# A forgetting-attention plus feed-forward kernel on Trainium2: splitting the second GEMM of chunk 0 over the attention of two batches

## The chip, the cores and the metric

The kernel runs on one core of one Trainium2 chip. The metric is device time in microseconds (us); lower is better. Every run named below computed the right result.

## The reference, cut to what matters

Eight batches of causal attention with a decay ("forget gate") are followed by a feed-forward block with an exact GELU. All inputs and outputs are float32.

```python
# q, k, v: (8 batches, 8 heads, 576 tokens, 64);  f: (8, 8, 576)
scores = q @ k.T / 8 + cum[:, :, :, None] - cum[:, :, None, :]   # cum = cumsum(log f)
attn   = softmax(where(causal, -1e9, scores))
x      = (attn @ v) -> (4608 tokens, 512)
h      = x @ w_in                       # 512 -> 2048, "first GEMM"
out    = gelu(h) @ w_out                # 2048 -> 512, "second GEMM"
```

## The kernel before

The kernel is a hand-made schedule: the order of the Python calls is the order of the instructions on each engine. A *chunk* is 512 of the 576 tokens of a batch (the 64-token tails of all batches form a ninth chunk at the end). For each batch there is an *attention* stage of 16 *score tiles* (four head pairs i, four tiles t), followed by the *first GEMM* of its chunk (16 blocks of four matmuls, each evacuated by a Gelu on ScalarE). The *second GEMM* of the chunk before is cut into *units* of one 128x128x512 matmul (or its equal) each, 64 in a chunk, and these fill the gaps of the attention.

In batch 0 and batch 1 q and k are transposed on TensorE (`transposes_pe`), and VectorE copies the result, eight copies for each group of two heads:

```python
    def transposes_pe(b, i, pool):
        ...                                   # 12 small matmuls into two PSUM tiles
        for which, ps in enumerate(pss):
            for h in range(2):
                ...
                for odd in range(2):
                    nc.vector.tensor_copy(rows[:, odd], ps[odd * D : (odd + 1) * D, h]...)
```

Batch 1 is attended with the second GEMM of chunk 0 as its filler. The lists give the number of units after each score tile:

```python
    FILL_1 = [[0, 4, 4, 0], [0, 2, 3, 3], [4, 4, 4, 4], [3, 3, 3, 3], [8, 0, 99]]

    def second_attention():
        b, fill, counts = 1, gemm2(0, True), FILL_1
        for i in range(HP):
            for t in range(4):
                scores(b, i, t)
                if i and t == 1:
                    attend(b, i - 1, 0, (0, 1, 2))
                ...                            # heads of pair i-1 at t = 2 and 3
                    if i < HP - 1:
                        x_dma(b, i - 1)        # x transposed by a DMA
                if (i, t) == (0, 2):
                    transposes_pe(1, 3, o_psum)
                if i == 1 and t in (0, 2):
                    weigh_v(1, 2 + t // 2)
                ...                            # loads of v and transposes of batch 2
                take(fill, counts[i][t])
        ...
```

The loads of w_out and the transposes of batch 1 stand in the first GEMM of chunk 0:

```python
        if b == 0:
            load_w_out(0)
            x_tail_dma(0)
        for ffb in range(0 if b else 4, n_ff):
            gemm1(b, ffb)
            if b == 0:
                if ffb in (7, 9, 15):
                    transposes_pe(1, (7, 9, 15).index(ffb), s_psum if ffb < 10 else o_psum)
                if ffb == 9:
                    weigh_v(1, 0)
                    for c in range(1, 4):
                        load_w_out(c)
                    load_qk_tokens(2)
                    weigh_v(1, 1)
            elif b + 1 < B:
                ...                            # copies and weighing for the next batch
```

The q,k of batch 1 are requested earlier, on the same GpSimd queue as w_in:

```python
        load_qk_tokens(1, 0, 4)
        load_w_in(2)
        load_w_in(3)
        load_qk_tokens(1, 4, 8)
```

The softmax here doesn't subtract the row's maximum and nothing guards it: scores larger than these inputs give would overflow.

## Time and profile before

| | kernel before |
|---|---|
| time, median of 3 runs | 356.26 us (354.95 to 357.58) |
| span of the profiled run | 356.0 us (an execution of 358.29 us) |
| first GEMM of chunk 0 starts | 26.66 us |
| attention of batch 1, with 64 units | 43.4 to 76.75 us |
| attention of batch 2, with 64 units | 90.66 to about 113.6 us |
| first score tile of batch 3 | 127.45 us |

The profile is one execution, and a slow one: at 358.29 us it lies above the three timed runs, with a mean granted clock of 0.986. Of the 38 fast runs of this kernel beside the experiments, the 20 at a clock of 0.993 or more average 354.2 us and the 6 at 0.986 or less 357.8 us. So the waits and the half clock of this trace need not be in every run. PE is TensorE, DVE VectorE, ACT ScalarE, POOL GpSimd, and SP issues many of the DMAs. A line of the timeline gives start and duration in us, engine, source line, operation, output<-input, and in brackets the idle time ahead of it with what ended that. A line of the waits gives engine and tile, the releaser, total us, number of waits, and the longest. The lines themselves stand in the prediction.

### The profile page before, as it was taken

The page shows a single profiled execution, that of the slowest core. Times are in us where ns is not written, and L with a number is a line of the kernel's source. Part 1 is how long each engine was busy: PE and PEld are TensorE (multiplying, and loading weights), DVE is VectorE, ACT ScalarE, POOL GpSimd, SP SyncE. Part 2 cuts the span into 40 slices and gives each one's busy share as a digit, 9 for nine tenths or more (in the row PEclk, how much of TensorE's full clock was granted, in tenths as well). Part 3 has the DMA queues.
Part 4 walks back from the last instruction along what each step waited for, and adds up shares of the span by engine and source line. Part 5 has one row for each costly group of instructions (what it writes and reads, how often), then busy time and mean ns, then how long its engine had stood idle before and what let it go on. Part 6 is the DMA issues. An engine that isn't in the chain of part 4 may idle for free.

```text
span 356.0 us, 7788 instructions
## 1 busy us (share of the span) xinstructions
PE 336.3 (94%) x3090; PEld 176.1 (49%) x3132; DVE 204.1 (57%) x503; ACT 215.1 (60%) x296; POOL 125.5 (35%) x245
## 2 busy tenths in 40 slices
PE   7698949999999999999999999999999999999995
PEld 3574523454555445544554455445544555444443
DVE  4561972579458955695669656974698363011011
ACT  5966563626874787478756876577647874603600
POOL 8291624334344424451446143705360430000000
PEclk9989996999999999999999999999999999999999
DMA  7899999955997779367945894389910121011013
GB/s 117 167 153 199 195 120 201 180 116 149 179 175 173 126 138 211 93 105 135 224 107 86 145 218 124 64 146 202 153 47 0 46 62 66 2 59 59 2 29 88
DMA packets 101219, 43.24 MB, mean 121 GB/s; under 512 B 80000, under 2 KB 96640, under 8 KB 101184
## 3 DMA queue, kind: packets, MB, share of 16 engines
q1 hardware_dynamic: 83888, 28.60, 40.2%
q0 software_dynamic: 16896, 13.63, 26.2%
q8 instruction: 24, 0.39, 0.5%
q10 hardware_dynamic: 400, 0.52, 0.4%
q14 instruction: 11, 0.09, 0.1%
HBM read 36.85 MB, written 9.44 MB: 130 GB/s over the span
## 4 chain that ended last, share of the span: by engine, by line
PE 76%; DMA 8%; ACT 7%; POOL 4%; SPq 3%; issue 2%; DVE 0%; POOLq 0%; ACTq 0%
PE ps L401 31%; PE ps L490 17%; PE ps L441 12%; PE o L338 9%; PE s L311 6%; DMA v_sb<-in_v_dram 4%; ACT e L317 4%; DMA w_out_sb<-in_moe_w_out_dram 4%; SPq L114 3%; ACT L317 2%; POOL vw L285 1%; ACT g L414 1%; PE ps_x L376 1%; POOL q L102 1%; POOL k L102 1%
## 5 line engine op out<-in xcount | busy, mean ns | idle before, releaser
L414 ACT ACTIVATE g<-ps 128x512 bf16<-128x512 f32 x144 | 85.8, 597 | 82.7 <-PE ps L401 82.7
L317 ACT ACTIVATE e<-s 128x896 bf16<-128x896 f32 (+1 forms) x128 | 103.8, 863 | 37.0 <-PE s L311 36.6
L401 PE MATMUL ps<-xT,w_in_sb 128*128 128x512 bf16 x503 | 111.8, 379 | 1.5 <-ACT g L414 1.0
L319 POOL TENSOR_SCALAR_AFFINE_SELECT e<-e 128x256 bf16<-128x256 bf16 x135 | 53.6, 406 | 123.9 <-ACT e L317 122.7
L490 PE MATMUL ps<-w_out_sb,g 64*128 64x512 bf16 (+1 forms) x666 | 96.2, 376 | 1.0
L401 PEld LDWEIGHTS <-w_in_sb 128*128 128x128 bf16 x576 | 56.0, 98 | 68.2 <-issue 3.0
L285 POOL TENSOR_TENSOR vw<-v_sb,wT 128x640 bf16<-128x640 f32 x32 | 40.9, 1279 | 41.8 <-DMA v_sb<-in_v_dram 25.7
L311 PE MATMUL s<-qT,kT 64*128 64x320 bf16 (+4 forms) x384 | 47.7, 285 | 3.7 <-ACT e L317 3.2
L490 PEld LDWEIGHTS <-g 64*128 64x128 bf16 (+1 forms) x690 | 37.7, 94 | 25.5 <-issue 1.6
L441 PE MATMUL ps<-w_out_sb,g 128*128 128x512 bf16 (+2 forms) x200 | 44.9, 371 | 5.4 <-DMA w_out_sb<-in_moe_w_out_dram 2.7
L338 PEld LDWEIGHTS <-e 128*128 128x128 bf16 x960 | 36.9, 100 | 18.8 <-issue 12.3
L338 PE MATMUL o<-vw,e 128*128 128x65 bf16 x960 | 42.9, 197 | 1.8 <-POOL vw L291 0.9
L269 DVE COPY qT<-tq 64x288 bf16<-64x288 bf16 x96 | 43.4, 452 | 1.5
L498 DVE COPY ot<-ps 128x512 f32<-128x512 f32 x24 | 16.5, 689 | 35.9 <-PE ps L490 35.9
L450 DVE COPY ot<-ps 128x512 f32<-128x512 f32 (+2 forms) x13 | 8.4, 650 | 48.9 <-PE ps L441 46.0
L269 DVE COPY kT<-tk 64x288 bf16<-64x288 bf16 x96 | 34.0, 354 | 1.6
L311 PEld LDWEIGHTS <-kT 64*128 64x128 bf16 x384 | 20.2, 94 | 28.6 <-issue 16.6
L353 DVE RECIPROCAL r<-o 128x5 f32<-128x5 f32 x64 | 12.5, 195 | 37.0 <-PE o L338 36.0
L441 PEld LDWEIGHTS <-g 128*128 128x128 bf16 x208 | 19.0, 99 | 24.2 <-issue 3.8
L354 DVE TENSOR_TENSOR x<-o,r 128x256 bf16<-128x256 f32 x64 | 27.2, 425 | 2.2
L364 DVE TENSOR_SCALAR xt<-o,r 64x64 bf16<-64x64 f32 x60 | 17.4, 291 | 1.4
L500 DVE TENSOR_TENSOR ot<-ot,ps 128x512 f32<-128x512 f32 x24 | 16.5, 688 | 1.3
(65 smaller groups left out, 146.9 us busy)
## 6 DMA issues: line engine op xcount, KB each, us to landing
out_dram<-ot SPq DMA_DIRECT2D x32, 256.0 KB, 2.4
v_sb<-in_v_dram SPq DMA_DIRECT2D x20, 256.0 KB, 4.9
v_sb<-in_v_dram SPq DMA_DIRECT2D x29, 128.0 KB, 5.7
q<-in_q_dram POOLq DMA_DIRECT2D x6, 576.0 KB, 6.1
k<-in_k_dram POOLq DMA_DIRECT2D x6, 576.0 KB, 8.7
w_in_sb<-in_moe_w_in_dram POOLq DMA_DIRECT2D x4, 512.0 KB, 8.6
w_out_sb<-in_moe_w_out_dram POOLq DMA_DIRECT2D x4, 512.0 KB, 16.4
q<-in_q_dram POOLq DMA_DIRECT2D x4, 144.0 KB, 4.4
```

The source lines that it names most:

```text
L269: nc.vector.tensor_copy(rows[:, odd], src[odd * D : (odd + 1) * D, 2 * i + h].rearrange("d j p -> d p j"),)
L285: nc.gpsimd.tensor_tensor(vw_of[b][:, hs, :, 0:D], v_sb[:, hs, :, :], w.unsqueeze(3).to_broadcast([P, 2, NBLK, D]), Alu.mult,)
L311: nc.tensor.matmul(to, *ab, start=half < 0, stop=half == 1 or not masked)
L317: nc.scalar.activation(et[:, :, 0:c], st[:, :, 0:c], Act.Exp, scale=scale)
L319: nc.gpsimd.affine_select(out=et[:, :, c0 : c0 + P], in_=et[:, :, c0 : c0 + P], compare_op=Alu.is_ge, fill=0.0, base=0, pattern=[[0, 2], [ ...
L338: nc.tensor.matmul(o[:, m, :], e_of[b, i, t][:, h, c : c + P], vw_of[b][:, 2 * i + h, n, :], start=(n == 0), stop=(n == m),)
L354: nc.vector.tensor_tensor(x_of[b, i][:, :, h, :], o[:, 0:4, 0:D], r[:, 0:4].unsqueeze(2).to_broadcast([P, NBLK - 1, D]), Alu.mult,)
L364: nc.vector.tensor_scalar(*tail, r[D:P, 4:5], None, Alu.mult)
L401: nc.tensor.matmul(ps, w_in_sb[:, kt, ffb * P : (ffb + 1) * P], src[:, kt, :], start=(kt == 0), stop=(kt == n_dm - 1),)
L414: nc.scalar.activation(g_of[c][ffb], ps, Act.Gelu)
L441: nc.tensor.matmul(pss[ts][:, c0:c1], g_of[c][kt][:, ts * P : (ts + 1) * P], w_out_sb[:, kt, c0:c1], start=(kt == 0), stop=(kt == n_ff - 1),)
L490: nc.tensor.matmul(banks[r], g_of[c][kt][rows, ts * P : (ts + 1) * P], w_out_sb[rows, kt, :], start=(kt == 0), stop=last if r else kt == n ...
```

## The change

The intent is to make the w_out load harmless. In batch 1 TensorE waits twice for w_out. The change leaves only a quarter of the second GEMM of chunk 0 there (16 units, late in the stage, needing half of w_out) and moves the other 48 units into batch 2. That allows q,k of batch 2 to be requested ahead of half of w_out. Around this several things move: v and w_in start earlier, q,k of batch 1 follow all of w_in, the transposes of batch 1 come later, x of batch 1 is transposed on TensorE instead of by DMA, and the first GEMM of chunk 1 gets the interleaved start that chunk 0 has.

```diff
-    FILL_1 = [[0, 4, 4, 0], [0, 2, 3, 3], [4, 4, 4, 4], [3, 3, 3, 3], [8, 0, 99]]
+    FILL_2 = [[8, 8, 8, 8], [8, 8, 4, 4], [4, 4, 4, 4], [4, 4, 4, 4], [8]]
+    FILL_1 = [[0, 0, 0, 0], [0, 0, 0, 0], [0, 0, 2, 2], [2, 2, 0, 0], [4]]
...
-        fill = gemm2_rows(b - 1)
+        fill = gemm2_third() if b == 2 else gemm2_rows(b - 1, PLAN)
...                                            # in the start of batch 0
+        weigh_v(0, 0, nc.vector)
...
-        load_qk_tokens(1, 0, 4)
         load_w_in(2)
         load_w_in(3)
+        load_qk_tokens(1, 0, 4)
         load_qk_tokens(1, 4, 8)
...                                            # in the attention of batch 1
-        b, fill, counts = 1, gemm2(0, True), FILL_1
+        b, fill = 1, gemm2_half(0, 0)
...
+                if (i, t) in ((0, 1), (1, 0)):
+                    transposes_pe(b, 2 + i, o_psum)
...
+                if i and t == 3:
+                    to_xT(b, i - 1, nc.vector.tensor_copy, o_psum, "o")
+                if (i, t) in ((1, 2), (2, 0)):
+                    weigh_v(1, i + 1)
...
+        both = s_psum.tile([P, 2, 1024], BF16, tag="s", name="ps_x2")
+        take(fill, 99)
+        gemm1_begin(1, both)
+        x_tail_dma(1)
+        transpose_dma(2, 0, 4)
         transpose_dma(2, 4, 8)
-        load_v(2, 4, 8)
-        take(fill, 999)
+        load_v(2)
...                                            # in the first GEMM of chunk 0
-            load_w_out(0)
             x_tail_dma(0)
...
-                if ffb in (7, 9, 15):
+                if ffb in (13, 15):
+                    transposes_pe(1, (13, 15).index(ffb), s_psum)
-                if ffb == 9:
+                if ffb == 12:
                     weigh_v(1, 0)
-                    for c in range(1, 4):
-                        load_w_out(c)
+                    load_w_out(0)
+                    load_w_out(1)
+                    weigh_v(1, 1)
                     load_qk_tokens(2)
-                    weigh_v(1, 1)
+                    load_w_out(2)
+                    load_w_out(3)
```

## The prediction

> **What bounds the kernel now.** I read the busy table and the chain of waits first. They name TensorE almost everywhere, so a change can gain only where TensorE stands idle or runs at half clock.
>
> ```profile
> PE 336.3 (94%) x3090; PEld 176.1 (49%) x3132; DVE 204.1 (57%) x503; ACT 215.1 (60%) x296; POOL 125.5 (35%) x245
> ...
> PE 76%; DMA 8%; ACT 7%; POOL 4%; SPq 3%; issue 2%; DVE 0%; POOLq 0%; ACTq 0%
> ```
>
> Next I cut the run into stages with the windows view. In a row stand the stretch, its length, each engine's busy time, then TensorE's granted clock, DMA share and GB/s.
>
> ```profile
> 26.66:43.40 16.74, 15.67 (x102) 7.85 (x102) 9.11 (x21) 10.61 (x18) 6.76 (x10) 1.00 1.24 196
> 43.40:76.75 33.35, 27.41 (x270) 13.25 (x273) 17.87 (x46) 16.27 (x19) 13.16 (x26) 0.90 1.11 158
> 76.75:90.66 13.91, 13.85 (x63) 6.16 (x65) 13.38 (x33) 8.96 (x15) 4.69 (x7) 1.00 0.65 147
> 90.66:113.71 23.05, 22.53 (x289) 13.18 (x293) 12.22 (x33) 16.06 (x19) 9.31 (x22) 1.00 1.07 187
> ```
>
> The rows are the first GEMM of chunk 0, the attention of batch 1 with the second GEMM of chunk 0, the first GEMM of chunk 1, and the attention of batch 2 with the second GEMM of chunk 1. Rows 2 and 4 hold nearly the same work (64 second-GEMM units each), yet row 2 takes 33.35 us against 23.05. These 10.3 us are all that this stage has to give. The waits of TensorE up to 130 us say what they are:
>
> ```profile
> PE ps L441 <- DMA w_out_sb<-in_moe_w_out_dram: 2.7, 1, 2.7
> PE s L311 <- ACT e L317: 2.1, 5, 0.7
> PE ps L441 <- ACT e L317: 2.0, 1, 2.0
> ```
>
> The second GEMM waits twice. The 2.0 us at 44 to 46.26 are put down to the exponential. But the first quarter of w_out was issued at 27.64 and the slowest landing of w_out took 18.6 us, which gives 46.2, so I read this as w_out too. After the second wait the clock falls: windows of 2 us show 0.70, 0.50, 0.50 and 0.60 from 52 to 60 us. The TensorE timeline shows two units in 1.01 us there, where five take 1.24 us at full clock:
>
> ```profile
> 53.75 1.01 PE L441 MATMUL ps<-w_out_sb,g 128*128 128x512 bf16 x2 [2.75 <-DMA w_out_sb<-in_moe_w_out_dram]
> ...
> 75.48 1.24 PE L441 MATMUL ps<-w_out_sb,g 128*128 128x512 bf16 x5
> ```
>
> **What the Trainium skill says.** "TensorE: Matmul & The Clock Gate", Part 1, has the array at half rate after an idle window of about 3.4 us and back at full rate after about 3.4 us of sustained work. The trace agrees on the two levels (0.50 and 1.00). It adds that light work is enough for the drop: the clock fell at 18 us after two windows of 2 us with 1.40 and 0.87 us busy, and after 53.75 us it took about 6 us to return. "Perfetto Trace Analysis", Identifying the Most-Contended Engine, warns that matmul busy time is no measure of headroom; so I compare stages of equal work instead of using the 94%. "VectorE: DVE Perf Modes", Why PSUM operands drop a tier, says that a PSUM source denies VectorE the fastest copy modes. The trace agrees in direction: a 64x288 copy takes about 479 ns from PSUM and 452 or 354 ns from SBUF. "DMA: Bandwidth & Descriptors", Issuing engines are not separate DMA queues, says that DMAs of all issuers interleave on the same 16 engines; the 193 to 204 GB/s that stays flat from 28 to 46 us agrees with a shared limit.
>
> **The change part by part.**
>
> 1. *The w_out waits go.* Batch 1 now runs 16 units (half the contraction of two row blocks), first after its eleventh score tile, near 62 us below, and they need only two quarters of w_out. Removed: 2.0 + 2.75 us of waiting, some 3 us of half clock (6 us at half rate), and 48 units.
>
> 2. *48 units move to batch 2.* One unit costs 0.2165 us (the first GEMM: 64 matmuls in 13.86 us). 48 x 0.2165 = 10.4 us, on the path, because row 4 is already dense (22.53 of 23.05 us). If they fill the 0.5 us left, +10.0 us. Break-even therefore needs batch 1 and its first GEMM to end 10.0 us earlier, at 80.7 instead of 90.66.
>
> 3. *The start.* v is requested about 1.5 us earlier, and VectorE weighs the first heads. But the first head now stands behind score tile (3,0). The exponential of (2,2) ended at 17.76; (2,3) and (3,0) follow, and the head can start near 18.3 instead of 17.58. Then VectorE's normalisation binds: four heads of 0.97, one copy of 0.42, four heads of 0.65 us make 6.9 us. From 19 to 19.3 this ends near 26; the first GEMM starts at 26.4 (estimate) instead of 26.66. Little is gained.
>
> 4. *The transposes of batch 1 come late.* They stood after GEMM blocks 7, 9, 15 and in the attention; they now stand after blocks 13 and 15 and twice in the attention. Their cost is not on TensorE (0.5 us each) but in the VectorE copies:
>
> ```profile
> 35.59 1.95 DVE L238 COPY qT<-s_t 64x288 bf16<-64x288 bf16 x4 [6.71 <-PE s_t L226]
> 37.56 1.98 DVE L238 COPY kT<-s_t 64x288 bf16<-64x288 bf16 x4
> ...
> 48.07 1.96 DVE L238 COPY qT<-ps_t 64x288 bf16<-64x288 bf16 x4 [0.60 <-PE ps_t L226]
> 50.06 1.96 DVE L238 COPY kT<-ps_t 64x288 bf16<-64x288 bf16 x4
> ```
>
> Eight copies take 3.93 us, all four groups 15.7 us. Before they ran from 35.6 to 52.0. Block 7 ended 34.88 - 26.66 = 8.22 us into the GEMM; six blocks of 0.866 us more give 26.4 + 13.4 = 39.8; the copies start 0.7 us after the transposes, at 40.5. The built program's waits show what hangs on them: the first score tile on group 0 (44.5), the third on group 1 (48.4), head 0 of batch 1 on half of group 3, and head 1 on all of it, because both use its PSUM banks. Group 2 runs from 48.6 to 52.6, group 3 to 56.6. So head 1 starts at 56.6, and score tile (1,2) stands behind it on TensorE.
>
> 5. *The rest of batch 1.* From (1,2) on, ten exponentials remain: 7 x 0.92 + 3 x 0.70 = 8.5 us, from 57.5 to about 66.9 with small gaps. Then the mask of the last tile (0.4 us on GpSimd and its wait), head 6 (0.6), 4 units (0.87), head 7 (0.6), 4 units (0.87): the first GEMM of chunk 1 starts at 70.4 us instead of 76.75, and with its own start (one transposed block 0.2, one wait on an evacuation 0.3) lasts 14.4 us and ends at 84.8. That is 5.9 us gained against 10.0 us paid: **+4.1 us**.
>
> 6. *The clock.* From 42.6 to 57 us TensorE has only about 5 us of real work in 14 us, lighter than what dropped the clock at 18 us. At half rate a pair of heads costs 2.0 instead of 1.25 us, four units 1.73 instead of 0.87, and exponentials wait behind them. Walking the same steps with half clock until about 65 us puts the start at 73.1 instead of 70.4. I give this three chances in four: **+2.0 us**. The sum is +6.1 us, 362.4; I take **361.8 us**, since a hand-walked chain may add waits that overlap.
>
> **The rivals.**
>
> *A: the w_out load was the whole trouble, and the change cures it.* For it: 4.75 us of waits and the half clock are real. With those alone gone and full filling kept, some 7 us, about 349 us. Against it: the change also takes 48 fillers out of a stage which then waits on VectorE and ScalarE. Even with an early GEMM start (25.0), head 1 stands at 55.2 and the same steps give 68.1, which ends near 358.
>
> *B: an even trade.* The removed waits balance the new idle time, 355 to 358 us: this needs the clock to stay up and the GEMM to start about 1 us earlier than I say.
>
> *C: late loads.* q,k of batch 1 now follow all of w_in on the GpSimd queue. If they land after 39.8, everything in step 4 slides along: 364 to 368 us. Against it: one w_out quarter has left the queue ahead, and v and w_in start earlier; the bytes at 195 GB/s give about 37.
>
> *D: batch 2 cannot take 112 units densely.* Its PSUM banks are evacuated by VectorE in 2 x 0.69 us. Against it: each row block ends where two heads follow, which cover this. At most 2 us.
>
> **Range and chances.** The sound end is 357 (step 5 without the clock, an early start), the bad end 367 (half clock throughout and late loads). 2% is 7.1 us, so 363.4 lies 1.6 us above my figure: slower by over 2% has 0.34, within 2% 0.63, faster 0.03.
>
> **What would show it.** Right: the first GEMM of chunk 0 starts at 26 to 27 us; copies of the batch 1 transposes run without a pause from about 40 to 56 us, and the first normalisation of batch 1 follows them; TensorE's clock is 0.5 in much of 45 to 62 us; no wait on w_out; the first GEMM of chunk 1 starts at 70 to 73.5 us; batch 2's attention lasts 33 us; from its end on the stages keep their 36.58 us. Wrong: copies that start before 38 us, a first GEMM of chunk 1 before 68 us, a clock that stays at 1.00, or a batch 2 shorter than 32 us.

## The result and the profile after

| | before | changed |
|---|---|---|
| median of 4 runs each | 356.48 us (354.95 to 357.58) | 367.4 us (366.73 to 371.95) |
| ratio | | 1.0345, 95% interval 1.0273 to 1.0416 |

The changed kernel is slower by 3.4%, above the range that was predicted. All outputs are right. Executions over 1.5% slower than the fastest of the same kernel are left out of the means. A ratio is the mean time of one kernel's fast runs over that of the other's fast runs, so it isn't quite the ratio of the medians; here it includes two further runs of the changed kernel (369.95 and 368.54 us). Three repeats of the pair on other chips gave 1.0433, 1.0391 and 1.0398. The first profile of the changed kernel happened to be taken in its slowest run (371.95 us); the repeats were used to see which of its waits are always there.

The busy line and the chain of waits on the changed kernel's page:

```profile
PE 341.6 (93%) x3128; PEld 178.9 (49%) x3169; DVE 206.5 (56%) x510; ACT 216.1 (59%) x297; POOL 124.5 (34%) x244
...
PE 78%; ACT 10%; DVE 4%; issue 3%; DMA 2%; POOL 1%; ACTq 0%; POOLq 0%; DVEq 0%
```

DMA's share of the chain fell from 8% to 2%, as intended: no wait on w_out is left. ScalarE's rose from 7% to 10% and VectorE's from 0% to 4%. TensorE is busy 5.3 us longer for nearly the same mathematics (it also transposes x of batch 1 now), at a mean granted clock of 0.972 instead of 0.986.

The stages of the changed kernel in the windows view (columns as in the prediction):

```profile
27.56:45.66 18.10, 15.24 (x91) 7.33 (x92) 5.39 (x14) 10.82 (x18) 7.25 (x10) 1.00 1.19 185
45.66:75.43 29.77, 21.73 (x238) 12.72 (x241) 20.07 (x51) 14.66 (x17) 8.75 (x20) 0.66 0.57 92
75.43:91.14 15.71, 14.40 (x68) 6.38 (x68) 9.06 (x28) 10.61 (x17) 0.00 (x0) 1.00 0.89 154
91.14:124.41 33.27, 32.18 (x364) 16.86 (x369) 21.53 (x46) 16.87 (x19) 18.45 (x35) 1.00 0.84 156
124.41:139.86 15.45, 14.02 (x65) 6.17 (x65) 12.52 (x34) 8.96 (x15) 3.87 (x6) 1.00 0.86 159
```

The second row is the attention of batch 1. It lost 48 of its 64 units, which are 10.4 us of full-rate work, yet became only 3.6 us shorter, at a mean clock of 0.66. The fourth row, batch 2, grew by 10.4 us. The third and fifth rows are the first GEMMs of chunks 1 and 2, which took 13.9 us each before. From the end of the fifth row on nothing changed: 356.0 - 127.45 and 368.4 - 139.86 are both 228.5 us.

TensorE's waits in the changed kernel up to 140 us, a selection of those that the kernel before does not have or has once less:

```profile
PE ps L401 <- ACT g L414: 2.0, 2, 1.0
PE s L311 <- DVE kT L238: 1.8, 1, 1.8
PE ps L401 <- DMA xT<-x: 1.4, 1, 1.4
...
PE o L338 <- DVE qT L238: 1.0, 1, 1.0
PE o L338 <- DVE kT L238: 0.9, 1, 0.9
```

Three of these are waits for VectorE's copies of q and k. The VectorE timeline shows them, first and last, and the first normalisation behind them:

```profile
41.67 1.95 DVE L238 COPY qT<-s_t 64x288 bf16<-64x288 bf16 x4 [11.89 <-PE s_t L226]
...
55.85 1.96 DVE L238 COPY kT<-ps_t 64x288 bf16<-64x288 bf16 x4
57.84 0.20 DVE L353 RECIPROCAL r<-o 128x5 f32<-128x5 f32 x1
```

VectorE had been idle for 11.89 us ahead of the copies and then copies almost without a pause until 57.8. Before, the same copies ran from 35.6 to 52.0. The clock, in windows of 2 us, first at its fall and then at its return:

```profile
46.00:48.00 2.00, 0.20 (x8) 0.07 (x3) 1.95 (x5) 1.71 (x2) 0.00 (x0) 0.96 1.14 179
48.00:50.00 2.00, 1.46 (x19) 1.22 (x19) 1.61 (x5) 1.13 (x2) 0.00 (x0) 0.50 1.30 207
...
66.00:68.00 2.00, 2.00 (x13) 0.88 (x12) 0.42 (x1) 0.70 (x1) 0.59 (x2) 0.50 0.00 0
68.00:70.00 2.00, 2.00 (x29) 0.97 (x28) 0.00 (x0) 1.83 (x2) 0.77 (x2) 0.92 0.00 0
```

TensorE runs at half rate from about 48 to 68 us.

The stretch from head 1 of batch 1 to the first GEMM of chunk 1, on TensorE's timeline: head 1, three waits between, and the GEMM.

```profile
57.87 1.01 PE L338 MATMUL o<-vw,e 128*128 128x65 bf16 x15 [0.91 <-DVE kT L238]
...
62.65 1.56 PE L338 MATMUL o<-vw,e 128*128 128x65 bf16 x25 [0.68 <-POOL e L319]
...
71.72 0.40 PE L376 MATMUL ps_x<-ident_bf,x 128*128 128x128 bf16 x4 [0.83 <-DVE x L354]
...
72.91 0.49 PE L338 MATMUL o<-vw,e 128*128 128x65 bf16 x10 [0.33 <-POOL e L319]
...
75.43 0.59 PE L401 MATMUL ps<-xT,w_in_sb 128*128 128x512 bf16 x2
```

Head 1 starts as soon as the last copy of kT ends. From there to the GEMM it takes 17.56 us, and 17.79, 16.92 and 17.08 us in the three later traces of this kernel.

### The profile page after: what moved, and what is told of

Its sections match the earlier page's. It is cut to its first block, busy times and chain, and to the rows that moved or that the text cites. A ratio compares the mean times of both kernels' runs of the same rounds, so it can differ in the third digit from the quotient of the medians.

```text
span 368.4 us, 7868 instructions
## 1 busy us (share of the span) xinstructions
PE 341.6 (93%) x3128; PEld 178.9 (49%) x3169; DVE 206.5 (56%) x510; ACT 216.1 (59%) x297; POOL 124.5 (34%) x244
## 4 chain that ended last, share of the span: by engine, by line
PE 78%; ACT 10%; DVE 4%; issue 3%; DMA 2%; POOL 1%; ACTq 0%; POOLq 0%; DVEq 0%
PE ps L401 33%; PE ps L489 18%; PE o L338 8%; PE ps L431 7%; PE s L311 7%; ACT e L317 6%; PE ps L524 2%; ACT L317 2%; ACT g L414 2%; DMA xT<-x 1%; DMA k<-in_k_dram 1%; DVE kT L238 1%; DVE qT L238 1%; PE ps_x L376 1%; DVE x L354 1%
## 5 line engine op out<-in xcount | busy, mean ns | idle before, releaser
L401 PE MATMUL ps<-xT,w_in_sb 128*128 128x512 bf16 x503 | 112.3, 379 | 4.1 <-ACT g L414 2.0
L489 PE MATMUL ps<-w_out_sb,g 64*128 64x512 bf16 (+1 forms) x726 | 103.3, 376 | 1.6 <-issue 0.8
L285 POOL TENSOR_TENSOR vw<-v_sb,wT 128x640 bf16<-128x640 f32 x31 | 39.6, 1278 | 46.4 <-DMA v_sb<-in_v_dram 32.4
L489 PEld LDWEIGHTS <-g 64*128 64x128 bf16 (+1 forms) x751 | 40.0, 94 | 30.9 <-issue 3.3
L269 DVE COPY qT<-tq 64x288 bf16<-64x288 bf16 x96 | 41.1, 428 | 4.8 <-DMA tq<-q 3.4
L497 DVE COPY ot<-ps 128x512 f32<-128x512 f32 x26 | 17.9, 690 | 42.9 <-PE ps L489 42.9
L269 DVE COPY kT<-tk 64x288 bf16<-64x288 bf16 x96 | 35.5, 370 | 3.3 <-DMA tk<-k 1.7
L440 DVE COPY ot<-ps 128x512 f32<-128x512 f32 (+2 forms) x9 | 5.7, 632 | 48.7 <-PE ps L431 46.0
L431 PE MATMUL ps<-w_out_sb,g 128*128 128x512 bf16 (+2 forms) x141 | 27.8, 355 | 0.2
L431 PEld LDWEIGHTS <-g 128*128 128x128 bf16 x144 | 13.5, 98 | 14.5
L499 DVE TENSOR_TENSOR ot<-ot,ps 128x512 f32<-128x512 f32 x26 | 17.9, 687 | 1.5
```

What stands on the lines that cost most here:

```text
L269: nc.vector.tensor_copy(rows[:, odd], src[odd * D : (odd + 1) * D, 2 * i + h].rearrange("d j p -> d p j"),)
L285: eng.tensor_tensor(vw_of[b][:, hs, :, 0:D], v_sb[:, hs, :, :], w.unsqueeze(3).to_broadcast([P, 2, NBLK, D]), Alu.mult,)
L401: nc.tensor.matmul(ps, w_in_sb[:, kt, ffb * P : (ffb + 1) * P], src[:, kt, :], start=(kt == 0), stop=(kt == n_dm - 1),)
L431: nc.tensor.matmul(pss[ts][:, c0:c1], g_of[c][kt][:, ts * P : (ts + 1) * P], w_out_sb[:, kt, c0:c1], start=(kt == 0), stop=(kt == n_ff - 1),)
L489: nc.tensor.matmul(banks[r], g_of[c][kt][rows, ts * P : (ts + 1) * P], w_out_sb[rows, kt, :], start=(kt == 0), stop=last if r else kt == n ...
L497: nc.vector.tensor_copy(ot, banks[1])
```

## The experiments

Eighteen runs of fifteen kernels were made in five groups. The kernels of a group shared a chip and the runs of the kernel before there. The runs of the kernel before scatter by 0.8 to 2% within a group (352.05 to 360.23 us over all groups), which makes much of the width of the intervals. (The 356.27 us of group 5 includes its one slow run; without it the median is 354.98 us.)

| group | kernel | median us | before, us | ratio [95%] | first GEMM of chunk 0 to first score tile of batch 3 |
|---|---|---|---|---|---|
| 1 | after_again | 369.19 | 353.78 | 1.0433 [1.0391, 1.0475] | 112.0 |
| 1 | early_copies | 365.48 | 353.78 | 1.0338 [1.0276, 1.0401] | 107.1 |
| 1 | warm_array | 366.68 | 353.78 | 1.0358 [1.0312, 1.0405] | 110.0 |
| 1 | tail_late | 352.31 | 353.78 | 0.9967 [0.9927, 1.0008] | 95.2 |
| 2 | only_units | 361.42 | 356.73 | 1.0138 [1.006, 1.0216] | 104.6 |
| 2 | weigh_early | 368.65 | 356.73 | 1.032 [1.0262, 1.0379] | 111.2 |
| 2 | fill_holes | 366.82 | 356.73 | 1.0283 [1.0206, 1.036] | 109.3 |
| 2 | old_start | 367.25 | 356.73 | 1.0289 [1.0225, 1.0352] | 110.9 |
| 3 | after_third | 369.1 | 355.82 | 1.0391 [1.0334, 1.0449] | 111.4 |
| 3 | holes_v2 | 366.4 | 355.82 | 1.0314 [1.0256, 1.0372] | 109.1 |
| 3 | plain_gemm1 | 368.43 | 355.82 | 1.038 [1.031, 1.0451] | 109.3 |
| 3 | tail_late_w1 | 353.51 | 355.82 | 0.9952 [0.9906, 0.9998] | 97.7 |
| 4 | after_fourth | 369.79 | 355.79 | 1.0398 [1.033, 1.0466] | 112.0 |
| 4 | early_plain | 365.51 | 355.79 | 1.0248 [1.0156, 1.034] | 109.0 |
| 4 | early_plain_old | 368.1 | 355.79 | 1.037 [1.0278, 1.0461] | 113.2 |
| 4 | only_units_2 | 360.68 | 355.79 | 1.0135 [1.0065, 1.0205] | 104.2 |
| 5 | early_plain_qk | 362.53 | 356.27 | 1.0219 [1.015, 1.0287] | 104.1 |
| 5 | early_plain_old_qk | 362.62 | 356.27 | 1.0216 [1.0131, 1.0301] | 106.8 |

The last column is read from each trace: it leaves out the start, which differs from run to run, and the unchanged end. It is 100.8 us in the kernel before and 112.3 in the first profile of the changed one. It is one execution of each kernel, so it shows which stage moved, while the times show by how much; the 100.8 us come from the slow execution named above.

The **theory** was that moving the units costs its 10 us in batch 2 and is not paid back in batch 1, because late copies and a half clock hold that stage. The **rivals** were that the first profile was of an odd run, that the units alone make the whole loss, and that the new start, the late loads or the new start of the first GEMM make it.

### The changed kernel again

No edit, three times.

> The changed kernel once more, for a second profile: the first was taken in the slowest of its runs (371.95 against 366.7 to 367.5 us). Expected 367 to 368 us. If the late first score tile (9.45 us against 7.56 before) belongs to that one run, the first GEMM of chunk 0 now starts near 26 us instead of 27.56. If it belongs to the change, it stays at 27 to 28. The wait of the first GEMM of chunk 2 on a transposed x (1.38 us) and the second wait on a Gelu (1.02 us) should be there again.

> The changed kernel unaltered, for a comparison on the same chip as the next two (its ratio to before was 1.0345 and 1.0433 on two chips). Expected ratio 1.03 to 1.045; stages of the trace as before: 18.1 to 18.3 us from the first GEMM of chunk 0 to batch 1, 33.3 us for batch 2's attention, 15.7 us for the first GEMM of chunk 1.

> The changed kernel unaltered, as the measure for its neighbours on this chip. From three earlier runs (ratios 1.0345, 1.0433, 1.0391): 367 to 370 us, 11 to 15 us more than the kernel before.

Measured: 369.19, 369.1 and 369.79 us, above the 367.4 of the first series on its own chip. The profile of the first repeat had the interleaved start's waits and the wait on transposed x (0.6 us). In the four traces of the changed kernel the first GEMM of chunk 0 starts at 27.56, 26.82, 27.37 and 26.18 us; from there to the first GEMM of chunk 1 they take 47.9, 48.3, 47.2 and 47.6 us. So the long middle is no accident, and the start varies by more than a microsecond.

### Only the units moved

The kernel before, with the 48 units moved and nothing else.

```diff
-    FILL_1 = [[0, 4, 4, 0], [0, 2, 3, 3], [4, 4, 4, 4], [3, 3, 3, 3], [8, 0, 99]]
+    FILL_1 = [[0, 0, 0, 0], [0, 0, 0, 0], [0, 0, 2, 2], [2, 2, 0, 0], [4, 0, 99]]
+    FILL_2 = [[8, 8, 8, 8], [8, 8, 4, 4], [4, 4, 4, 4], [4, 4, 4, 4], [8]]
...
-        b, fill, counts = 1, gemm2(0, True), FILL_1
+        b, fill, counts = 1, gemm2_half(0, 0), FILL_1
...                                            # and the generators of these units
```

> The kernel before with only the 48 units of the second GEMM of chunk 0 moved from batch 1 to batch 2; start, load order, transposes and the start of each first GEMM stay as before. Theory (the unit move is nearly an even trade: 48 x 0.2165 = 10.4 us more in batch 2, and batch 1 loses its w_out waits, its half clock and 48 units, but is then bound by exponentials and heads): batch 2's attention 33 us, batch 1 to the first GEMM of chunk 1 some 40 us instead of 50, the time within 3 us of before. Rival (the unit move alone is what costs): 8 us or more above before.

> The kernel before with only the 48 units moved, again, on this chip as the measure for the two kernels beside it: 1.0138 times the kernel before, some 361 us, in the earlier run.

Measured: +4.7 and +4.9 us by the medians, 1.4% both times. That is more than the 3 us of the theory and far from the rival that it is the whole loss. Batch 2 took 33.26 us, as in the changed kernel. The first GEMM of chunk 0 and the attention of batch 1 together took 42.9 and 42.6 us instead of 50.1, not the 40 that were expected, so 7.2 to 7.5 us came back, against some 10.4 paid. The timeline of TensorE in the first of these runs shows what kept batch 1 from shrinking further:

```profile
54.12 0.27 PE L338 MATMUL o<-vw,e 128*128 128x65 bf16 x3 [1.97 <-POOL e L319]
```

Without units between them, the heads meet masks that GpSimd had not made yet. The clock also fell to 0.50 in windows of both runs.

### The copies of batch 1 in their old places

```diff
-                if (i, t) in ((0, 1), (1, 0)):
-                    transposes_pe(b, 2 + i, o_psum)
+                if (i, t) == (0, 2):
+                    transposes_pe(b, 3, o_psum)
...
-                if ffb in (13, 15):
-                    transposes_pe(1, (13, 15).index(ffb), s_psum)
+                if ffb in (7, 9, 15):
+                    transposes_pe(1, (7, 9, 15).index(ffb), s_psum if ffb < 10 else o_psum)
```

> The changed kernel with one part undone: the four transposes of batch 1 stand again after GEMM blocks 7, 9, 15 and after score tile (0,2). Theory (VectorE's copies of these transposes hold back the heads of batch 1): copies run from 36.5 to 53 instead of 41.7 to 57.8, head 1 of batch 1 starts near 53 instead of 57.9, and the time falls by 4 to 5.5 us, to 362 to 363. Rival (the units moved to batch 2 and the clock are all of it): below 1.5 us.

Measured: 3.7 us faster than the unaltered changed kernel of its group, a little less than expected; the first GEMM of chunk 1 started at 69.68 instead of 75.14 us. The mechanism holds. The copies did not start at 35 as before, though, but at 37.3, because TensorE waited 1.13 us for k. This is the first sign of the load order, taken up below.

### The clock held up

Idle matmuls on a zero tile were put between the score tiles of batch 1. They are 35 by the edit and in the trace; the expectation's 47 is a miscount.

```diff
+        WARM = [[9, 3, 3, 3], [0, 5, 0, 0]]
+        warm_up(7)
...
+                if i < 2 and WARM[i][t]:
+                    warm_up(WARM[i][t])
...
+                    if i == 1:                 # between heads 0 and 1
+                        warm_up(5)
```

> The changed kernel with 47 idle 128x512 matmuls in the holes of batch 1 up to head 1 (results unused), to hold TensorE's clock up. Theory (half clock from 47 to 68 us costs some 3 us because heads, score tiles and units stand in one line behind each other): clock 1.00 from 45 to 75, the first GEMM of chunk 1 starts 2 to 3.5 us earlier, 364 to 365 us. Rival (the stage waits for VectorE and ScalarE whatever the clock): within 1 us of the changed kernel.

Measured: 2.5 us faster than the unaltered kernel of the group by the medians. The granted clock stayed at 1.00 until about 62 us, fell to 0.50 and was back before 68. The half clock is therefore a real cost, but its size is less clear than the time says. From the first GEMM of chunk 0 to that of chunk 1 the trace took 47.1 us against 48.3 in the unaltered kernel of the group, so 1.2 us and not the expected 2 to 3.5. Another 0.8 us is the absent wait on a transposed x, which comes and goes without the edit (see the last group). From head 1 to the GEMM it took 16.0 us instead of 16.9 to 17.8. The late copies remained, and so did most of the loss.

### The first GEMM of chunk 1 started plainly

```diff
-        both = s_psum.tile([P, 2, 1024], BF16, tag="s", name="ps_x2")
         take(fill, 99)
-        gemm1_begin(1, both)
+        to_xT(1, HP - 1, nc.vector.tensor_copy, o_psum, "o")
...
-        for ffb in range(0 if b > 1 else 4, n_ff):
+        for ffb in range(0 if b else 4, n_ff):
...                                            # untangle and weigh_v only for at >= 0
```

> The changed kernel with the plain start of the first GEMM of chunk 1 as in the kernel before (last transposed block first, then the blocks in order) instead of the interleaved one. Theory (the interleaved start costs a wait on Gelu of 1.02 us and one on an evacuation of 0.24 us): that GEMM takes 13.9 instead of 15.7 us, against a wait of up to 0.8 us ahead of it; 0.8 to 1.5 us less in the trace, at the edge of what the clock can tell. Rival: the wait ahead of it eats all, no change.

Measured: this GEMM took 14.40 instead of 15.71 us, and the wait on transposed x before the next GEMM was absent in its profile. In time it was 0.7 us faster by the median, which three rounds do not resolve.

### The old start

The start of batch 0 as before (v weighed by GpSimd alone, heads ahead of score tile (2,3)).

```diff
-        weigh_v(0, 0, nc.vector)
-        gate = x_pool.tile([P, 1], FP32, tag="gate", name="gate")
...
+        for i in range(HP):
+            weigh_v(0, i)
+            if i < 2:
+                load_w_in(i)
...
-        scores(0, 2, 3)
-        scores(0, 3, 0)
         attend_head(0, 0)
-        scores(0, 3, 1)
+        scores(0, 2, 3)
```

> The changed kernel with the old start: v loaded behind the masks' constants, all four weighings on GpSimd, heads of batch 0 after the third score tile of pair 2 as before. Traces so far: from the first score tile to the first GEMM 17.9 to 18.1 us in the changed kernel (20.05 once, with a late load), 19.1 and 16.4 in two of the old start. Theory (the new start gains nothing): within 1.5 us of the changed kernel, either way. Rival (the new start costs 1.5 us or more): 1.5 us or more faster.

Measured: 367.25 us, 1.0289, on a chip where the unaltered changed kernel did not run; its interval overlaps those of three of the four series of that kernel. The profile started its first GEMM at 27.34 us after a stretch of half clock at 15 to 21 us. This is inconclusive; a cleaner pair follows in the last group.

### The masks of the late heads

`weigh_v(1, 2)` and `weigh_v(1, 3)` go from the attention to right behind the loads of w_out.

```diff
                     load_w_out(2)
                     load_w_out(3)
+                    weigh_v(1, 2)
+                    weigh_v(1, 3)
```

> The changed kernel with the last two weighings of v for batch 1 issued on GpSimd right after the w_out loads instead of between the masks of batch 1. Theory (TensorE waits 1.0 us for masks that stand behind a weighing of 1.5 us on GpSimd): the wait of head 2 on the mask goes from 0.7 to under 0.2, 1 to 1.5 us less. Rival (another wait takes its place): no change.

Measured: the wait of 0.68 us for a mask is gone, and from head 0 of batch 1 to the first GEMM of chunk 1 it takes 18.0 us instead of 18.8 to 19.7. In time (1.032) it cannot be told from the changed kernel.

### Sixteen more units into the holes of batch 1

32 units in batch 1, the first of them in the holes ahead of its heads; in the second form v of batch 2 is also requested early.

```diff
-    FILL_2 = [[8, 8, 8, 8], [8, 8, 4, 4], [4, 4, 4, 4], [4, 4, 4, 4], [8]]
-    FILL_1 = [[0, 0, 0, 0], [0, 0, 0, 0], [0, 0, 2, 2], [2, 2, 0, 0], [4]]
+    FILL_2 = [[4, 4, 4, 4], [8, 8, 4, 4], [4, 4, 4, 4], [4, 4, 4, 4], [8]]
+    FILL_1 = [[0, 0, 0, 4], [4, 4, 0, 0], [0, 0, 2, 2], [2, 2, 0, 0], [4]]
...                                            # both halves of two row blocks, both evacuated by ScalarE
...                                            # second form only
+                if (i, t) == (2, 0):
+                    load_v(2)
```

> The changed kernel with 32 instead of 16 units in batch 1: the first 16 stand in the holes before head 1, the other 16 where the change has its 16; batch 2 has 96 instead of 112. Theory (batch 1 has idle TensorE to take them, and they hold the clock up): batch 2's attention 29.8 instead of 33.3 us, the first GEMM of chunk 1 starts no later or up to 1.5 us earlier, 3.5 to 5 us less than the changed kernel. Rival (each unit in batch 1 lengthens it as much as it shortens batch 2): no change.

> The kernel with 32 units in batch 1 (fill_holes), with v of batch 2 loaded as soon as batch 1 has weighed its v, instead of behind the transposes at its end. In fill_holes batch 2's attention stayed at 33.04 us with 96 instead of 112 units: TensorE waited for masks that stood behind the late weighings of v on GpSimd. Theory (the late v load is a hidden second bound of batch 2): batch 2's attention 29.8 to 30.2 us, no wait on a mask over 0.3 us there, the wait on a transposed x at the first GEMM of chunk 2 gone, 3.5 to 5 us faster than fill_holes was against the changed kernel. Rival (batch 2 does not shrink with fewer units for another reason): 33 us again.

Measured: 1.0283 and 1.0314. The second form was 2.7 us faster than the unaltered kernel of its group. In both the units did fit into batch 1 without making it longer (45.7 and 45.0 us between the first GEMMs of chunks 0 and 1), but batch 2 did not give back the 3.5 us that 16 units take (33.04 and 32.47 us instead of 29.8). A new wait took their place each time. In the first form the last v of batch 2 came so late that GpSimd weighed it inside batch 2 and was late with the masks (TensorE timeline):

```profile
97.92 0.24 PE L338 MATMUL o<-vw,e 128*128 128x65 bf16 x2 [1.33 <-POOL e L319]
```

In the second form the weighing was done in time, but the DMA transposes of q and k for batch 2 now met the load of q,k of batch 3. The timeline of SP, with the time that it took to issue two of them:

```profile
79.75 5.24 SPq L255 DMA_TRANSPOSE tq<-q  x1
...
85.04 4.42 SPq L255 DMA_TRANSPOSE tk<-k  x1
```

In the changed kernel these take 1.3 to 2.2 us. TensorE then waited 1.67 and 0.41 us for kT at the start of batch 2. Both expectations of a shorter batch 2 missed.

### What had made the kernel before wait for w_out

Two edits of the kernel before. The small DMA transpose of the tails of batch 0 moves from behind the first w_out load to the end of batch 1; in the second form the second quarter of w_out is also requested right behind the first.

```diff
             load_w_out(0)
-            x_tail_dma(0)
+            load_w_out(1)                     # second form only, no longer requested later
...
         to_xT(b, i, nc.vector.tensor_copy, o_psum, "o")
+        x_tail_dma(0)
         x_tail_dma(b)
```

> The kernel before with one step moved: the small DMA transpose of batch 0's tail rows is issued at the end of batch 1 instead of ahead of it. In the trace of before the DMA rate falls from about 195 to 77 and 38 GB/s between 48 and 52 us, just when that transpose runs and while w_out is awaited. Theory (the transpose stops the w_out loads): the wait on w_out of 2.75 us and the half clock after it go, 350 to 353 us. Rival (w_out is simply last in a long queue): 355 to 357 us.

> A version that may beat both: the kernel before with the tail transpose of batch 0 issued at the end of batch 1, and the second quarter of w_out requested right behind the first. tail_late alone gave 0.9967 of before (0.9927 to 1.0008), with one wait on w_out of 1.6 us left. Theory: that wait goes, the clock stays at 1.00, 1 to 2% faster than before. Rival (v and q,k of batch 1 come later by the half megabyte put ahead of them, and something else waits): no gain.

Windows of the kernel before around its waits on w_out, and of the first form (the last column is GB/s):

```profile
48.00:50.00 2.00, 1.68 (x21) 0.81 (x19) 1.89 (x4) 1.11 (x2) 0.00 (x0) 1.00 2.55 77
50.00:52.00 2.00, 0.66 (x10) 0.39 (x10) 1.93 (x5) 1.91 (x3) 0.77 (x2) 1.00 0.24 38
```

```profile
48.00:50.00 2.00, 1.33 (x22) 0.57 (x16) 1.93 (x5) 1.77 (x3) 0.18 (x1) 1.00 1.25 205
50.00:52.00 2.00, 2.00 (x30) 1.11 (x30) 1.55 (x5) 1.64 (x3) 2.00 (x5) 1.00 1.24 205
```

The rate had fallen to 38 GB/s while this transpose was under way (it landed 16.0 us after its issue), and stays at 205 without it. In the two kernels with only the units moved, where the transpose stands in its old place, the rate fell to 77 and 65 GB/s as well. In the first form the second wait, 2.75 us, is gone, and the clock stays at 1.00 from 40 to 70 us. The first unit still waits 1.6 us, now by the trace for w_out, which landed 18.2 us after its issue. So the theory holds for the second wait and the rival for the first, and the prediction's reading of the first wait as w_out is borne out. In the second form the first unit waits 2.0 us and the clock falls to 0.57 between 46 and 50 us; both of these expectations missed. The time gained is small: 0.9967, with an interval that includes no gain at all, and 0.9952 [0.9906, 0.9998], 2.3 us by the medians. The expected 350 to 353 us was met in time by the level of this chip more than by a gain, since the kernel before was itself at 353.8 there. The second form is told apart from the kernel before, barely and by less than 2%; the first is not.

The trace of the first form is 5.6 us shorter than that of the kernel before in the stretch to batch 3, its time only 1.5 us. The trace of the kernel before is of an execution of 358.29 us, 4.5 us above the median of this group's runs of that kernel, which would account for the difference; no second trace of it was kept.

### Undoing several parts together

Four kernels settle whether the parts add, and what the loads cost. `early_plain` is the changed kernel with both the early transposes and the plain first GEMM. `early_plain_old` has the old start too. The two `_qk` forms also request q,k of batch 1 where the kernel before did:

```diff
+        load_qk_tokens(1, 0, 4)
         load_w_in(2)
         load_w_in(3)
-        load_qk_tokens(1, 0, 4)
         load_qk_tokens(1, 4, 8)
```

> The changed kernel with two parts undone: the transposes of batch 1 back in their early places, and the first GEMM of chunk 1 started plainly. Theory that the terms add: early copies alone gave -3.7 us and the plain GEMM -0.7 us by time (-5.5 and -1.3 us by the stages of their traces), so together 4.4 to 6.8 us below the unaltered kernel of this chip, some 362.5 to 365. Rival, that both meet the same idle time (the GEMM's wait on a Gelu would only move elsewhere): no more than the 3.7 us of early copies alone, 365 or above.

> The same with the old start as well, so that of the change there remain the 48 moved units, the order and places of the loads, and the attention of batch 1 without transposed x by DMA. Theory that the start costs about 1 us and the rest adds: 1 us below early_plain, within 2 us of only_units_2. Rival, that the late loads cost something of their own (q,k of batch 1 behind w_in, w_out late, v of batch 2 late): 4 us or more above only_units_2.

Measured for these two: 365.51 us, 4.3 us below the unaltered kernel of the group (5.3 by the ratios), at the low end of adding; and 368.1 us, 7.4 us above the kernel with only the units moved, which is the rival's result: something else costs. The traces name it. TensorE's timeline of `early_plain`, at the first transposes of batch 1:

```profile
36.31 0.43 PE L226 MATMUL s_t<-ident_bf,q 96*128 96x96 bf16 x6 [0.49 <-DMA q<-in_q_dram]
38.34 0.43 PE L226 MATMUL s_t<-ident_bf,k 96*128 96x96 bf16 x6 [1.60 <-DMA k<-in_k_dram]
```

In `early_plain_old` the first GEMM started at 25.29 us, the earliest of this group, and TensorE then waited 1.93 us for q and 1.60 for k; its first score tile of batch 1 stood at 48.99 us, no earlier than in `early_plain` (48.30). Behind these waits the clock fell to 0.50, so the same GEMM took 21.1 and 23.7 us instead of 17. Whatever is early ahead of this point is lost at it.

> early_plain (transposes of batch 1 early, first GEMM of chunk 1 plain) with one more part undone: q,k of heads 0 to 3 of batch 1 are again requested ahead of the last two quarters of w_in. Theory that the late q,k load is what held early_plain back (its trace shows TensorE waiting 0.5 and 1.6 us for q and k, then half clock, and 21.1 us from the start of the first GEMM to the first score tile against 17.0 in the kernel with only the units moved): these waits are gone, the stage takes 17.0 to 17.5 us, the time falls by 3 to 4 us to about 1.013 to 1.018 times the kernel before, some 361 to 362.5. Rival, that the later places of w_out and v loads or the new start hold it: less than 1.5 us from early_plain's 1.0248.

> The same with the old start. In early_plain_old the first GEMM began at 25.29 us and the gain was lost again in waits of 1.9 and 1.6 us for q and k. Theory that only the q,k load held it: within 1.5 us of the kernel with only the units moved (1.0135 and 1.0138), and not above early_plain_qk; an estimate of 1 us less for the old start is within what three rounds resolve. Rival, that the late w_out and v loads cost something of their own: 2 us or more above the kernel with only the units moved, with waits on w_out or on transposed x of 1 us or more.

Measured: 362.53 and 362.62 us. With the old request order TensorE's timeline of `early_plain_qk` shows no wait at the same place:

```profile
35.31 0.42 PE L226 MATMUL s_t<-ident_bf,q 96*128 96x96 bf16 x6
35.57 0.42 PE L226 MATMUL s_t<-ident_bf,k 96*128 96x96 bf16 x6
```

The stage took 16.8 us, the first GEMM of chunk 1 started at 69.60 instead of 74.07, and the first score tile of batch 3 came 5.0 us earlier. In time it is 3.0 us below `early_plain` by the medians, as expected, but only 0.3% by the ratios, less than expected (the kernel before ran at 352.6 to 357.1 us in its fast runs of that group). The waits and the stage are settled; the size in time is between 1 and 3 us. The old start made no difference in time (0.1 us): the new start neither gains nor costs anything that these rounds resolve. The profile with the old start has a wait of 1.94 us on a transposed x that the other lacks, so a difference of that size could be hidden.

By the medians `early_plain_old_qk` still lies 1.2 and 1.9 us above the two runs of the kernel with only the units moved, between its theory and its rival; by the ratios it is 0.8%, some 2.8 us, which is the rival's result. Its profile has a wait of 1.94 us on transposed x, of the kind that the rival named, ahead of the first GEMM of chunk 2, and the profile of `early_plain_qk` none. That wait is in all four traces of the changed kernel (1.38, 0.6, 1.1 and 1.35 us), and the SP timelines show its origin. First the kernel before, then the changed one:

```profile
87.67 11.32 SPq L114 DMA_DIRECT2D v_sb<-in_v_dram  x5
...
109.68 1.22 SPq L382 DMA_TRANSPOSE xT<-x  x1
```

```profile
99.82 11.09 SPq L114 DMA_DIRECT2D v_sb<-in_v_dram  x5
...
121.76 1.95 SPq L382 DMA_TRANSPOSE xT<-x  x1
```

v of batch 3 is requested about 12 us later. In the changed kernel v of batch 2 is requested only after batch 1, GpSimd waits for it (19.66 us of idle time until 92.51) and weighs it inside batch 2, and only then is the buffer free for v of batch 3. The DMA transposes of x stand behind that load on SP. Before, the last one was issued 3.9 us ahead of the GEMM that reads it (113.55 us), now 2.7 us ahead (124.41). That the late v causes the wait follows from this order in the traces, and `holes_v2` supports it: there v of batch 2 came early and the wait was gone. With the late v it hangs on how long SP takes to issue the load of v: 9.21 to 9.38 us in the three kernels without the wait (`plain_gemm1`, `early_plain_qk`, `warm_array`), 9.51 and 9.73 us with a wait of 0.42 and 0.6, and 11.0 to 11.5 us in the others with waits of 1.0 to 1.9 (in `fill_holes` the view doesn't separate this load). So the absence of this wait in `plain_gemm1` and `warm_array` was not their edits' doing.

## Why the prediction was wrong

The direction was right, and so were the units' cost, the late copies and the fall of the clock. The size was not: the time on record was 361.8 us, at most 367, and the changed kernel took 367.4 to 369.8. The likeliest outcome was put at "within 2%" (0.63), and slower by over 2% at 0.34; it was slower by 3.4 to 4.3%. What failed in the mechanism is step 5, the walk from head 1 of batch 1 to the first GEMM of chunk 1, and the sentence that the later stages stay as they are. Compared with the unrounded sum of 362.4, the traces of the changed kernel show these terms.

1. **The w_out waits go** (step 1): right. None is left (`tail_late` bears out that the first of them was for w_out). But "some 3 us of half clock" did not go away. It grew, from part of 52 to 60 us to 48 to 68 us.

2. **48 units move to batch 2, +10.0 us** (step 2): right. The stage grew from 22.9 to 33.27 us, +10.4.

3. **"Little is gained" at the start, 26.4 us** (step 3): right in substance. It was 26.2 to 27.6 us in four traces, 0.6 us later on average than written. With the loads restored, the old and the new start came out at 362.62 and 362.53 us, though the first may hide a gain behind a wait.

4. **The transposes come late** (step 4): right, and shown. The copies ran from 41.7 to 57.8 us where 40.5 to 56.6 had been walked, head 1 started 30.3 to 30.5 us after the first GEMM of chunk 0 where the walk has 30.2, and undoing their places gave back 3.7 us. Rival C, that q,k land after 39.8, did not happen. But the runs showed a link that the prediction missed: q,k are late enough (TensorE waited for k until 36.9 to 38.3 us in the kernels that use them earlier) that the late places are only 2 to 4 us behind what the loads allow. The step treated the place as a free choice and the loads as a separate rival; they are one cost.

5. **"The first GEMM of chunk 1 starts at 70.4 us ... lasts 14.4 us"** (step 5): **this step failed**. The GEMM started at 73.8 to 75.4 us, 47.2 to 48.3 us after the first GEMM of chunk 0 instead of 44.0. The loss lies behind head 1: from it to the GEMM the walk has 13.8 us, and 16.5 at half clock; measured are 16.9 to 17.8, and still 16.0 in `warm_array`, where the clock was held for most of it. The step ran the ten exponentials "with small gaps", in 9.4 us. In the first trace they took 12.9 us, 8.4 us busy as written and 4.5 idle: the score tiles stand on TensorE behind heads, units and transposes, and these waited 0.68 and 0.33 us for masks and 0.83 us for a normalised x. `weigh_early` removed the 0.68, and from head 0 to the GEMM it took 18.0 us instead of 18.8 to 19.7. How the rest divides between these waits and the clock stays open. The waits of 1.79 and 2.35 us at the first two score tiles are not part of it, since head 1 came as walked. The GEMM lasted 15.7 us. The walk had a transposed block and an evacuation in its start (0.2 and 0.3 us, measured 0.22 and 0.24), but not the wait of 1.0 us for a Gelu, which the first GEMM of chunk 0 shows in the same way. With the plain start it took 14.4 us.

6. **"Half clock until about 65 us", +2.0 as three quarters of 2.7** (step 6): the mechanism is right, and the half clock came in all four traces, until 68 us. With it in full, the walk gives 46.7 us from GEMM to GEMM, and 47.2 to 48.3 were measured. The size of 2.7 us is not shown: holding the clock until 62 us gave 2.5 us in time, but 1.2 us in the stage.

7. **"From its end on the stages keep their 36.58 us"**: wrong for the next stage. The first GEMM of chunk 2 took 0.8 to 1.6 us longer, for the wait on transposed x. The prediction did not follow the late request of v through GpSimd to SP. That this is the cause is argued from the order in the traces; the changed kernel with only v early was not run.

8. **"I take 361.8 us, since a hand-walked chain may add waits that overlap"**: this correction went the wrong way. The walk had left waits out.

9. Two sums don't come out. In rival A a start at 25.0 instead of 26.4 gives 69.0 us, not 68.1, so an end near 359. And the "sound end" of 357 is not reached by what it names: without the clock the sum is 360.4, with the start at 25.0 still 359.0.

The sum closes. With the means of the four traces one adds to 362.4: 0.6 for the start (27.0 instead of 26.4), 1.8 for the stretch between the two GEMMs (47.8 instead of 46.0), 1.3 for the GEMM of chunk 1, 0.4 for batch 2 and 1.3 for the GEMM of chunk 2. That makes 367.8 us, against 367.4 to 369.8 measured. It is good to about 2 us only, since it is added to a median of 356.3 us while the trace of before took 358.29. The bad end of 367 had half clock and late q,k loads. The clock came and q,k did not delay the transposes; five other terms of 0.4 to 1.8 us, which the walk had left out or cut short, all lay on the bad side (0.7 of the 1.8 is the last quarter of step 6's clock).

As to the loss as a whole, the experiments give this account of the stretch to batch 3: 100.8 us before, 104.2 and 104.6 with the units alone, 104.1 when the changed kernel gets back its transposes, plain GEMM and q,k order (106.8 with the old start too, 2.0 of it the wait on transposed x), and 112 as changed. So about a third of the loss (3.4 to 3.8 us) is the trade of units itself, and two thirds are what was moved around it. In time, on the one chip that ran both, the units alone cost 4.9 us of 14.0. What stays open is the sharp division between late copies, q,k order and clock, which act on each other: the parts undone alone gave 3.7 us for the copies, 2.5 for the clock and 0.7 for the plain GEMM, the q,k order was undone only together with the first and the last, and the kernel before alone scatters by up to 7 us within a group.

## What to carry to other kernels

Work that fills gaps is free only where it fills them: moved to a stage that is already dense it costs its full duration (10.4 us for 48 units), and the stage that it leaves becomes shorter only as far as the next waits there allow. Before a consumer is moved later, or a load behind another, one follows both to the last wait that they release: here the late q,k limited how early the transposes could stand, the transposes set the copies and the copies the heads, and the clock fell in the thin work between. A walk by hand leaves waits out and so errs to one side: here five terms of 0.4 to 1.8 us all came out long, and a range should add such terms up on that side. And a trace is one execution: where a kernel's runs scatter, one looks where in them the traced one lies.

## What the Trainium skill lacked or had wrong

- "TensorE: Matmul & The Clock Gate", Part 1, names idle windows, sustained work and short gaps between groups of matmuls, but gives no figure for how little work lets the clock fall. In the changed kernel it fell after two windows of 2 us with 0.34 and 0.20 us busy. In `warm_array` it fell after one with 1.33, within one with 1.07, while in `tail_late` two with 1.23 and 1.13 passed at 1.00; so no busy share decides it. In the changed kernel it then stayed at 0.50 through ten windows, most of them 1.05 to 1.74 us busy.
- "DMA: Bandwidth & Descriptors", Rules for kernel authors, says that a transpose next to ordinary DMAs needs nothing. That is about correctness; it costs time. One small transpose of tails issued after the first w_out load held SP for 5.74 us and landed after 16.0 us, and the rate fell to 38 GB/s meanwhile; with it moved the rate was 205. It is not always so: in the changed kernel the same transpose was issued 1.4 us ahead of w_out, landed after 6.5 us, and the rate stayed at 144 GB/s or more. Two transposes of q and k beside a load took 5.24 and 4.42 us to issue instead of 1.3 to 2.2.
- "ScalarE: Activation LUTs", What ACT_TABLE_LOAD costs, gives about 2.66 us for a switch, of which the drain is more than half. In the kernel before the load at 44.04 us took 1.28 us and the exponential started 0.02 us after it; no drain of that size is seen, at most the 0.43 us of idle time ahead of the load.
